# Attention and a routed expert layer on one core: GpSimd's two-operand work waits for VectorE's, row lists come by one copy each, and the plan has new dates

## The chip, the cores and the metric

One Trainium2 chip; the kernel runs on one of its cores. Five engines work beside each other: TensorE (PE, with its weight loads apart as PEld), VectorE (DVE), ScalarE (ACT), GpSimd (POOL) and SyncE (SP, which issues most transfers). The metric is the device time of one execution in microseconds; of several runs the median counts.

## The reference

Attention over 8 batches, 12 heads, 448 tokens and 64 features, with q and k normalised, and then a mixture of 16 experts (4 groups of 4), each token going to one of them:

```python
q_n, k_n = rmsnorm(q, g_q), rmsnorm(k, g_k)
scores = scale * q_n @ k_n.T
attn = softmax(scores)
x = (attn @ v).transpose(0, 2, 1, 3).reshape(3584, 768)
g, e = argmax(x @ w_group), argmax(x @ w_expert[g])      # one expert for each token
out[t] = g_w[t] * e_w[t] * (relu(x[t] @ w1[g, e]) @ w2[g, e])   # 768 -> 1024 -> 768
```

All inputs and the output are float32.

## The kernel before

Every float32 operand of a matmul is carried as a high and a low 16-bit half, and the product is made of three 16-bit matmuls. So behind each tile stands a subtraction that makes the low half, in which two operands lie in SBUF. These are the operations that the change is about:

- `pl` (L619, in `plan_scores`): the low half of the exponentials, 128x896 for two score blocks, on POOL, in some places on DVE. There are 11 for each of the 16 units, 12 for the first (a unit is half a batch, six heads).
- `vl` (L374, `v_lo`): the low half of v, 128x768, twice for each unit, always on DVE.
- `kn` (L298, `k_lo`), on POOL or DVE; `xhl` (L731, in `plan_finish`), on POOL, for the last units also on DVE; `w1l` and `w2l` (L1389, `w_split`), the low halves of the experts' weights, on DVE.
- in the router's `choices` a chain of small operations on DVE and POOL (`rc`, `rd`, `row` and others).

The attention part takes 16 units through preparation (`plan_prep`), the rows' maxima (`mx`, L534, a DVE reduction of PSUM), scores and exponentials, the product with v (`po`, L664) and a store to `x16`. Token groups are routed between units, and `put` (L1067) writes each token into its expert's list `tab`. Then come jobs of up to 352 tokens of an expert each: POOL copies the rows of the list (`rows`, L1401, L1406, L1410) and gathers the tokens by them (`xg`, L1424), SP transposes them (`mx<-xg`), PE runs `mm1` (L1435) and `mul2` (L1462), and POOL scatters the result (L1481).

The order of work comes from a table. `Flow.add` lists some 2,700 tasks with their dependencies and the buffers that they take; `PLAN` gives each task a date (hundredths of a us; a star puts the task on the second of its two engines), and `Flow.emit` writes the tasks out by date. Each engine then runs its instructions in that order and waits only for data and buffers. The table reaches over the attention part and the first 10 of 18 jobs; the later jobs are dated from it by `Moe.plan`. The dates are an order and no times of the chip.

A list's last block of 64 or 32 tokens is worked on by all 128 partitions: the rows are copied 2 or 4 times under each other, each copy a DMA of its own from POOL:

```python
for q in range(r):
    nc.gpsimd.dma_start(t[q * m:q * m + m, i], self.tab[bass.ds(s + a, m)])
```

Of the kernel before, what the change touches and what calls it, by code (L numbers as in the profile page):

```python
# [63 lines left out]

class Flow:
# [40 lines left out]

    def emit(self, agenda, step):
        at = agenda.at(0)
        for t in self.order():
            at(t.start / step, (lambda t=t: t.f(t.on)) if len(t.engines) > 1 else t.f)  # L110


class Attention:
# [129 lines left out]
    def plan_prep(self, flow, u, B, D):  # L243

        nc = self.nc
# [7 lines left out]
        add = flow.add  # L253
# [127 lines left out]
        else:  # L381
# [16 lines left out]
            for a, e in KV:  # L398
# [4 lines left out]
                kl.append(add(both, lambda g, a=a, e=e: k_lo(g, a, e), [kh], uses=[B["nk"], B["kn"]]))  # L403
# [11 lines left out]
            x = add("POOL", lambda: self.one_row(nc.gpsimd, 0, 0), takes=[B["kb"]]) if u == 3 else None  # L415
# [14 lines left out]
            x = add("POOL", lambda: self.max_row(0, 0), takes=[B["qb"]]) if u == 3 else None  # L430
# [4 lines left out]
        for a, e in ((0, V // 2), (V // 2, V)):  # L435
# [4 lines left out]
            D["v"].append(add("DVE", lambda a=a, e=e: v_lo(a, e), [hi, *D["v"]],  # L440
                              takes=[B["vl"]] if a == 0 else (), uses=[B["nv"], B["vh"]] + ([B["vl"]] if a else [])))
# [138 lines left out]
    def plan_scores(self, flow, u, B, D):  # L580
# [42 lines left out]
        for a, e in self.pairs_of(N, u):  # L623
# [7 lines left out]
            x = flow.add(on, lambda g, a=a, e=e: lo(g, a, e), [x], uses=[bp])  # L631
# [77 lines left out]
    def plan_finish(self, flow, u, B, D):  # L709
# [23 lines left out]
        def st():  # L733
# [8 lines left out]
        y = flow.add(["POOL", "DVE"][::-1 if u == self.U - 1 else 1], lo, [x],  # L742
                     uses=[B["xm"], B["hl"]])
# [3 lines left out]
    def plan(self, flow, router, order):  # L747
# [52 lines left out]
        self.final = add("DVE", lambda: order.final(router.bank), done, takes=[Buffer("psx")])  # L800


class Router:
# [462 lines left out]
class Moe:  # L1266
# [222 lines left out]
    def plan_early(self, flow, attn, router, opens):  # L1489
# [15 lines left out]
        def weights(k):  # L1505
            ks = k if k < 2 else k - 2
            for i in range(len(PC)):
# [363 lines left out]
```

## Time and profile before

| | |
|---|---|
| runs | 1018.06 us median of 3, 1016.33 to 1020.02 |
| profiled execution | 1023.34 us, its span 1021.7 us |
| mean granted TensorE clock | 0.971 |
| busy share of the span | PE 89%, DVE 73%, ACT 60%, POOL 56% |

The shares are means over two unlike halves. Up to about 500 us, in the attention part, DVE and POOL are busy nearly all the time; from 650 us PE is, in the experts' part. A busy engine need not be working: the time in which an instruction has begun and is held up counts as its duration.

### The profile page before, as it was taken

What the parts mean: (1) busy time and instruction counts of PE and PEld (TensorE: products, weight loads), DVE (VectorE), ACT (ScalarE), POOL (GpSimd) and SP (SyncE); (2) the same over time, 40 slices, a digit from 0 to 9 for tenths busy, and PEclk for the clock granted to TensorE, in tenths of its full rate; (3) what the DMA queues carried; (4) which work ended last, traced back from release to release, by engine and by line L of the source; (5) the groups of instructions that cost most, each with busy time, mean ns of one, the idle gap of its engine ahead of it and who ended that gap; (6) DMA issues with size and microseconds to landing.
All of it is one profiled execution on the core that took longest, in us unless ns stands there. A gap on an engine that the chain in (4) does not pass through costs nothing.

```text
span 1021.7 us, 28764 instructions
## 1 busy us (share of the span) xinstructions
PE 913.6 (89%) x11761; PEld 651.9 (64%) x11761; DVE 746.2 (73%) x1002; ACT 617.9 (60%) x952; POOL 577.2 (56%) x490
## 2 busy tenths in 40 slices
PE   2789889999999798987987999899898999999995
PEld 1446556566666465655865866577776687778883
DVE  4999988999999999999754465456657585756520
ACT  4789688788888676666642364446446455546520
POOL 7379798899999798887645333223112231434311
PEclk9999899999999899999998999899999899999998
DMA  5756767787779667556998889799988899998910
GB/s 140 199 150 164 169 165 174 167 196 191 185 145 206 147 167 143 103 114 199 229 213 270 218 278 260 237 332 300 264 261 304 295 242 268 344 269 287 296 51 27
DMA packets 223095, 213.77 MB, mean 209 GB/s; under 512 B 129456, under 2 KB 179622, under 8 KB 222961
## 3 DMA queue, kind: packets, MB, share of 16 engines
q1 hardware_dynamic: 213008, 188.23, 70.6%
q0 software_dynamic: 8608, 22.99, 7.2%
q8 instruction: 93, 1.52, 0.7%
q10 hardware_dynamic: 1344, 0.69, 0.3%
q14 instruction: 42, 0.34, 0.1%
HBM read 145.69 MB, written 23.41 MB: 166 GB/s over the span
## 4 chain that ended last, share of the span: by engine, by line
PE 38%; DMA 19%; DVE 15%; POOL 11%; issue 7%; ACT 6%; SPq 3%; POOLq 0%; DVEq 0%; ACTq 0%
PE ps L1462 15%; PE ps L1435 14%; POOL pl L619 6%; DVE mx L534 5%; DMA xg<-x,tb 5%; DMA mx<-xg 4%; DMA stage<-w 3%; PE po L664 3%; PE pss L603 3%; DVE vl L374 2%; ACT p L613 2%; POOL xhl L731 1%; DMA nq<-q 1%; DVE ss L267 1%; DMA nk<-k 1%
## 5 line engine op out<-in xcount | busy, mean ns | idle before, releaser
L619 POOL TENSOR_TENSOR pl<-p 128x896 f16<-128x896 f32 (+1 forms) x161 | 269.9, 1698 | 40.4 <-ACT p L613 39.8
L1435 PE MATMUL ps<-mx,w1h 128*128 128x256 f16 (+6 forms) x1728 | 248.9, 260 | 21.0 <-DMA mx<-xg 13.9
L1435 PE MATMUL ps<-mx,w1l 128*128 128x256 f16 (+6 forms) x864 | 214.4, 260 | 0.3 <-DVE w1l L1389 0.3
L613 ACT ACTIVATE p<-pss 128x896 f32<-128x896 f32 (+1 forms) x177 | 152.4, 882 | 71.5 <-PE pss L603 54.8
L1435 PEld LDWEIGHTS <-w1h 128*128 128x128 f16 x1728 | 156.8, 99 | 42.3 <-issue 23.7
L534 DVE TENSOR_REDUCE mx<-pmx 128x2 f32<-128x896 f32 (+1 forms) x177 | 174.9, 1033 | 8.5 <-PE pmx L524 4.7
L664 PEld LDWEIGHTS <-p 128*128 128x128 bf16 (+1 forms) x3072 | 144.7, 103 | 52.0 <-issue 37.6
L664 PE MATMUL po<-vh,pl 128*128 128x65 f16 (+1 forms) x1536 | 156.9, 197 | 15.4 <-POOL pl L619 14.8
L1462 PE MATMUL ps<-w2h,hl 128*128 128x384 f16 (+2 forms) x768 | 163.9, 304 | 0.8 <-DVE hl L1444 0.8
L1462 PE MATMUL ps<-w2h,hh 128*128 128x384 f16 (+2 forms) x768 | 164.6, 306 | 0.0
L1462 PE MATMUL ps<-w2l,hh 128*128 128x384 f16 (+2 forms) x768 | 164.1, 304 | 0.0
L664 PE MATMUL po<-vh,p 128*128 128x65 f16 (+1 forms) x1536 | 159.3, 200 | 3.2 <-DVE nk L283 1.2
L664 PE MATMUL po<-vl,p 128*128 128x64 f16 (+1 forms) x1536 | 157.6, 196 | 0.0
L1389 DVE SCALAR_TENSOR_TENSOR w2l<-stage,w2h 128x1536 f16<-128x1536 f32 x64 | 111.5, 1753 | 63.0 <-ACT w2h L1387 63.0
L664 PEld LDWEIGHTS <-pl 128*128 128x128 f16 (+1 forms) x1536 | 128.6, 103 | 18.5 <-POOL pl L619 17.6
L1389 DVE SCALAR_TENSOR_TENSOR w1l<-stage,w1h 128x1536 f16<-128x1536 f32 x64 | 112.3, 1777 | 36.8 <-ACT w1h L1387 36.8
L1462 PEld LDWEIGHTS <-hh 128*128 128x128 f16 (+2 forms) x1536 | 101.4, 101 | 57.7 <-issue 6.0
L1481 POOL DMA_INDIRECT out<-y,tb x23 | 35.4, 1539 | 179.7 <-ACT y L1474 76.5
L1442 ACT ACTIVATE hh<-ps 128x256 f16<-128x256 f32 (+6 forms) x144 | 47.2, 347 | 126.0 <-PE ps L1435 111.3
L1387 ACT ACTIVATE w1h<-stage 128x1536 f16<-128x1536 f32 x64 | 93.5, 1479 | 46.4 <-DMA stage<-w 46.1
L1424 POOL DMA_INDIRECT xg<-x,tb x41 | 61.0, 1487 | 105.3 <-DMA mx<-xg 61.4
L603 PE MATMUL pss<-qa,kt 128*128 128x448 f16 x288 | 105.2, 365 | 9.4 <-DVE mx L534 5.0
(208 smaller groups left out, 1611.9 us busy)
## 6 DMA issues: line engine op xcount, KB each, us to landing
stage<-w SPq DMA_DIRECT2D x64, 768.0 KB
stage<-w SPq DMA_DIRECT2D x64, 512.0 KB
stage<-w SPq DMA_DIRECT2D x64, 256.0 KB
vn<-v SPq DMA_DIRECT2D x16, 576.0 KB
x<-xhl SPq DMA_DIRECT2D x16, 576.0 KB
nk<-k SPq DMA_DIRECT2D x30, 288.0 KB
nq<-q SPq DMA_DIRECT2D x30, 288.0 KB
qa<-qh SPq DMA_DIRECT2D x30, 176.0 KB
```

The source lines that it names most:

```text
L534: nc.vector.tensor_reduce(d["mx"][:, a:ns[-1] + 1:step], d.pop(("mm", a))[:, 0:len(ns), 0:448], axis=AX.X, op=ALU.max)
L603: nc.tensor.matmul(s[:, n - a, 0:448], w[:, n * P:(n + 1) * P], mv[:, x:z], start=first, stop=not first)
L613: nc.scalar.activation(p[:, 0:e - a], s, AF.Exp, scale=1.0 / 64)
L619: ENG[eng].tensor_tensor(l[:, 0:n], p[:, 0:n], h[:, 0:n], op=ALU.subtract)
L664: nc.tensor.matmul(o[op, c, 0:nn], w, mv, start=st, stop=sp, skip_group_check=True)
L1387: self.nc.scalar.activation(hi, t, AF.Copy, scale=64.0)
L1389: self.nc.vector.scalar_tensor_tensor(lo, t, 64.0, hi, op0=ALU.mult, op1=ALU.subtract)
L1424: self.nc.gpsimd.indirect_dma_start(g[0:m], None, self.x16[0:n], bass.IndirectOffsetOnAxis(ap=tb[0:m, i, 0:1], axis=0), bounds_check=n - 1 ...
L1435: nc.tensor.matmul(s[:, 0:c], wb[w][:, i, fs], x[:, l + i, o:o + c], start=i + j == 0, stop=i == DC - 1 and j == 2)
L1442: self.nc.scalar.activation(hh, s[:, 0:c], AF.Relu)
L1462: nc.tensor.matmul(s[q * m:q * m + m, 0:n], self.h[h][:, f, a:a + m], wb[w][:, f, o:o + n], start=f + j == 0, stop=f == self.FC - 1 and j ...
L1481: i = self.nc.gpsimd.indirect_dma_start(out, bass.IndirectOffsetOnAxis(ap=idx, axis=0), d.pop(("y", i))[:, 0:self.D // r], None, bounds_ch ...
```

## The change

First, some 360 tasks are marked with `port`: those of POOL with two operands in SBUF, and DVE's of the same kind (`pl`, `vl`, `kn`, `xhl`, the weights' low halves of the planned jobs, some of the router's steps). When `emit` writes out a marked task of DVE, it keeps its last DVE instruction; the next marked task of POOL in the plan then waits by semaphore for that one. One DVE operation is waited for once, and DVE waits for nothing more than before. In the plan 50 tasks of POOL get such a wait, all in the attention part.

Second, a list's last rows come by one copy whose source names them r times. Over the program the copies of such blocks become 18 in place of 50 (8 at L1401, 42 at L1410).

Third, all dates of `PLAN` are new, and with them the order on every engine. By the stars, 10 `pl` of 128x896 and two pairs of `xhl` go from POOL to DVE, and one `kn` of 128x448 from DVE to POOL. The task that sorts the experts (`order.final`) needs only the router's last step in the plan, and no longer the `put`s behind it.

```diff
@@ class Flow
+    def shared(self, task):
+        task.port = True
+        return task
+
     def emit(self, agenda, step):
-        at = agenda.at(0)
+        at, tc = agenda.at(0), self.tc
+        sync = mybir.DependencyInfo(mybir.DependencyClass.Sync, mybir.DependencyReason.SCHED_ONLY)
+        seen, held = [], []
+        def run(t):
+            del seen[:]
+            tc.nc.push_inst_callback(lambda i, *_, **__: seen.append(i))
+            t.f(t.on) if len(t.engines) > 1 else t.f()
+            tc.nc.pop_inst_callback()
+            if t.port and t.on == "DVE":
+                held[:] = [i for i in seen if i.engine == mybir.EngineType.DVE][-1:]
+            elif t.port and held:
+                i = next(i for i in seen if i.engine == mybir.EngineType.Pool)
+                tc.add_manual_dep(i, held.pop().name, sync, reason="one of the two at a time")
+
         for t in self.order():
-            at(t.start / step, (lambda t=t: t.f(t.on)) if len(t.engines) > 1 else t.f)
+            at(t.start / step, lambda t=t: run(t))
...
@@ plan_scores
-            x = flow.add(on, lambda g, a=a, e=e: lo(g, a, e), [x], uses=[bp])
+            x = flow.shared(flow.add(on, lambda g, a=a, e=e: lo(g, a, e), [x], uses=[bp]))
...
@@ Attention.plan
-        self.final = add("DVE", lambda: order.final(router.bank), done, takes=[Buffer("psx")])
+        self.final = add("DVE", lambda: order.final(router.bank), done[:1], takes=[Buffer("psx")])
...
@@ Router.plan
+            x.port = on == "POOL" or j in (1, 3, 5, 6, 12, 15, 18)
...
@@ Moe.rows
-                for q in range(r):
-                    nc.gpsimd.dma_start(t[q * m:q * m + m, i], self.tab[bass.ds(s + a, m)])
+                self.copies(t[:, i], self.tab[bass.ds(s + a, m)], r)
...
-            for q in range(r):
-                nc.gpsimd.dma_start(t[q * m:q * m + m, i], tab[:, a:a + m].rearrange("o p t -> p (o t)"))
+            self.copies(t[:, i], tab[:, a:a + m].rearrange("o p t -> p (o t)"), r)
+
+    def copies(self, dst, src, r):
+
+        m = src.shape[0]
+        self.nc.gpsimd.dma_start(dst, src.unsqueeze(0).to_broadcast([r, m, 2]))
...
 PLAN = """
-210 487 1965 426 1206 1507 11957 13909 2150 1783 2461 0 1 424 485 486 550 849 915 1020 1207 1508 2149* 2354 2567 1444
+210 487 2972 1086 1206 1517 10553 13066 13060 916 3554 0 1 424 485 474 550 731 915 1020 1085 1469 1534* 1779 1898 1442
...
```

POOL in the attention part, where the scores of unit 10 are made (`pl10_2` is its block 2; `p3210_2` the exponentials that it reads; what an instruction waits for stands in brackets). Before:

```order
L619 TENSOR_TENSOR pl10_2_6587<-p3210_2_6586 128x896 [waits Activation_49,Pool_49]
L619 TENSOR_TENSOR pl10_0_6623<-p3210_0_6622 128x896 [waits Activation_49]
L619 TENSOR_TENSOR pl10_10_6657<-p3210_10_6656 128x896 [waits Activation_49]
L619 TENSOR_TENSOR pl10_6_6685<-p3210_6_6684 128x896 [waits Activation_49,Pool_49]
L619 TENSOR_TENSOR pl10_8_6632<-p3210_8_6631 128x896 [waits PE_49]
```

The same place of POOL in the changed kernel:

```order
L637 TENSOR_TENSOR pl10_2_6499<-p3210_2_6498 128x896 [waits DVE_49,Activation_49,Pool_49]
L1084 DMA tab_58<-row_241,slot0_5421 59392x2 [waits DMASW1_49]
L637 TENSOR_TENSOR pl10_4_6630<-p3210_4_6629 128x896 [waits DVE_49,Activation_49]
L637 TENSOR_TENSOR pl10_10_6637<-p3210_10_6636 128x896 [waits Activation_49]
L1084 DMA tab_58<-row_241,slot0_5421 59392x2 [waits DMASW2_49]
L637 TENSOR_TENSOR pl10_8_6686<-p3210_8_6685 128x896 [waits Activation_49]
L749 TENSOR_TENSOR xhl9_6760<-xm9_6363,xhl9_6760 128x3x384 [waits DMAHW5_49,DMAHW4_49,DMAHW6_49,DVE_49,Activation_49]
```

Before, `pl` followed `pl` with no wait for DVE. Now three of these rows wait for DVE, blocks 0 and 6 are gone to DVE, and over the whole program 70 rows of POOL name DVE among their waits, in place of 30.

DVE at the same place, around the first `vl` of unit 11 and the end of unit 9. Of the kernel before:

```order
L283 TENSOR_TENSOR nk13_5953<-nk13_5953,po0_111 128x448
L669 TENSOR_SCALAR rr9_2_6680<-po1_112 128x7
L670 RECIPROCAL rr9_2_6680<-rr9_2_6680 128x7
L534 TENSOR_REDUCE mx11_6590<-pmx11_17_6645 128x1
L374 SCALAR_TENSOR_TENSOR vl11_6687<-vn1_134,vh2_132 128x768
L534 TENSOR_REDUCE mx11_6590<-pmx11_14_6689 128x2
```

And of the changed kernel:

```order
L392 SCALAR_TENSOR_TENSOR vl10_5977<-vn0_133,vh1_131 128x768
L706 TENSOR_TENSOR xm9_6363<-po0_111,rr9_1_6483 128x2x3x64
L707 TENSOR_TENSOR xm9_6363<-po0_111,rr9_1_6483 128x64
L392 SCALAR_TENSOR_TENSOR vl11_6578<-vn1_134,vh2_132 128x768
L637 TENSOR_TENSOR pl10_0_6518<-p3210_0_6517 128x896
L296 SCALAR_TENSOR_TENSOR ss13_6266<-ss13_6266,po0_111 128x42
```

The `vl` of unit 11 stands earlier, behind the `xm` of unit 9, and a `pl` follows it that was POOL's.

POOL where the rows of job 1 are fetched (`tb1`; 224 rows are blocks of 128, 64 and 32), before:

```order
L1406 DMA tb1_9544<-tab_58 128x2 [waits DMASW4_49]
L1410 ISA
L1410 DMA tb1_9544<-tab_58 64x2 [waits DMASW5_49]
L1410 ISA
L1410 DMA tb1_9544<-tab_58 64x2 [waits DMASW6_49]
L1410 ISA
L1410 DMA tb1_9544<-tab_58 32x2 [waits DMASW7_49]
L1410 ISA
L1410 DMA tb1_9544<-tab_58 32x2
```

and now:

```order
L1423 DMA tb1_9575<-tab_58 128x2 [waits DMASW4_49]
L1431 ISA
L1431 DMA tb1_9575<-tab_58 128x1x2 [waits DMASW5_49]
L1431 ISA
L1431 DMA tb1_9575<-tab_58 128x1x2 [waits DMASW6_49]
```

Two copies are left of the six for the blocks of 64 and 32 rows (the first piece goes on for two more copies), each over all 128 partitions.

## Rows read from the trace of the kernel before

**Rows 1.** The page, part 1: busy us, share of the span, instructions.

```profile
PE 913.6 (89%) x11761; PEld 651.9 (64%) x11761; DVE 746.2 (73%) x1002; ACT 617.9 (60%) x952; POOL 577.2 (56%) x490
```

**Rows 2.** Three stretches: length, busy PE PEld DVE ACT POOL, clock, DMA share, GB/s.

```profile
50.00:500.00 450.00, 402.05 (x6707) 265.75 (x6706) 420.49 (x568) 346.08 (x588) 389.85 (x279) 0.97 0.72 165
500.00:650.00 150.00, 135.32 (x1553) 101.60 (x1552) 79.90 (x138) 67.67 (x104) 62.93 (x61) 0.96 0.88 249
650.00:1000.00 350.00, 341.89 (x3222) 263.14 (x3220) 210.09 (x240) 173.21 (x214) 94.63 (x83) 0.98 0.90 267
```

**Rows 3.** The chain that ended last, 50 to 500 us, shares by line.

```profile
by line: POOL pl L619 14.7%; DVE mx L534 10.3%; issue 7.1%; PE po L664 6.8%; PE pss L603 5.8%; DVE vl L374 3.5%; ACT p L613 3.4%; POOL xhl L731 3.0%; POOL tab L1067 2.2%; DMA qb<-ql 2.1%; POOL kn L298 2.1%; DMA qa<-qh 1.8%; DVE ss L267 1.6%
```

**Rows 4.** DVE in order of time, 322 to 345 us: start, us, what.

```profile
324.24 0.95 DVE L374 SCALAR_TENSOR_TENSOR vl<-vn,vh 128x768 f16<-128x768 f32 x1
...
330.96 8.04 DVE L374 SCALAR_TENSOR_TENSOR vl<-vn,vh 128x768 f16<-128x768 f32 x1
```

**Rows 5.** POOL in order of time, 326 to 345 us.

```profile
326.48 9.86 POOL L619 TENSOR_TENSOR pl<-p 128x896 f16<-128x896 f32 x6
336.31 1.87 POOL L298 TENSOR_TENSOR kn<-nk,kn 128x896 f16<-128x896 f32 x1
338.34 1.52 POOL L1067 DMA_INDIRECT tab<-row,slot  x1 [0.16 <-issue]
343.94 1.68 POOL L619 TENSOR_TENSOR pl<-p 128x896 f16<-128x896 f32 x1 [4.08 <-ACT p L613]
```

**Rows 6.** DVE in order of time, 98 to 113 us, the second long `vl`.

```profile
103.53 6.20 DVE L374 SCALAR_TENSOR_TENSOR vl<-vn,vh 128x768 f16<-128x768 f32 x1
```

**Rows 7.** DVE in order of time, 394 to 408 us, the third.

```profile
395.98 1.08 DVE L619 TENSOR_TENSOR pl<-p 128x896 f16<-128x896 f32 x1
...
398.17 5.62 DVE L374 SCALAR_TENSOR_TENSOR vl<-vn,vh 128x768 f16<-128x768 f32 x1
```

**Rows 8.** The chain, pieces from 394 to 408 us.

```profile
398.00 7.33 POOL pl L619 x4
```

**Rows 9.** DVE's groups, 50 to 500 us: count, busy us, mean ns, idle before.

```profile
L374 DVE SCALAR_TENSOR_TENSOR vl<-vn,vh 128x768 f16<-128x768 f32 x31 | 59.7, 1924 | 0.0
...
L619 DVE TENSOR_TENSOR pl<-p 128x896 f16<-128x896 f32 x13 | 16.9, 1304 | 0.7 <-ACT p L613 0.7
...
L731 DVE TENSOR_TENSOR xhl<-xm,xhl 128x1152 f16<-128x1152 f32 x2 | 4.2, 2110 | 0.0
```

**Rows 10.** POOL's groups, 50 to 500 us.

```profile
L619 POOL TENSOR_TENSOR pl<-p 128x896 f16<-128x896 f32 x146 | 254.2, 1760 | 38.4 <-ACT p L613 37.9
L731 POOL TENSOR_TENSOR xhl<-xm,xhl 128x1152 f16<-128x1152 f32 x13 | 31.7, 2436 | 0.2 <-ACT xhl L727 0.2
...
L731 POOL TENSOR_TENSOR xhl<-xm,xhl 128x192 f16<-128x192 f32 x13 | 10.0, 770 | 0.0
```

**Rows 11.** POOL in order of time, 455 to 660 us.

```profile
460.39 0.98 POOL L1180 CAST first<-oof 1x2 int32<-1x2 f32 x1 [0.20 <-DVE oof L1178]
...
532.27 3.47 POOL L1401 DMA_DIRECT2D tb<-tab  x6 [2.15 <-DMA tab<-row,slot]
539.76 1.13 POOL L1424 DMA_INDIRECT xg<-x,tb  x1 [4.01 <-DMA tb<-tab]
...
568.29 2.27 POOL L1410 DMA_DIRECT2D tb<-tab  x4
...
614.51 2.02 POOL L1410 DMA_DIRECT2D tb<-tab  x4
```

**Rows 12.** POOL's groups over the span, the copies of row lists.

```profile
L1410 POOL DMA_DIRECT2D tb<-tab x42 | 22.1, 539 | 2.8 <-DMA out<-y,tb 1.7
L1406 POOL DMA_DIRECT2D tb<-tab x16 | 9.7, 603 | 0.7 <-issue 0.4
...
L1401 POOL DMA_DIRECT2D tb<-tab x8 | 4.2, 532 | 2.5 <-DMA tab<-row,slot 2.1
```

**Rows 13.** Who waited for whom on POOL: us in total, times, longest.

```profile
POOL xg L1424 <- DMA tb<-tab: 6.5, 2, 4.0
```

More of the change, by code (lines that the diff above doesn't have):

```diff
@@ L402, in plan_prep @@
                          takes=[B["kn"]] if a == 0 else (), uses=[B["nk"]] + ([B["kn"]] if a else []))
-                kl.append(add(both, lambda g, a=a, e=e: k_lo(g, a, e), [kh], uses=[B["nk"], B["kn"]]))
+                kl.append(flow.shared(add(both, lambda g, a=a, e=e: k_lo(g, a, e), [kh], uses=[B["nk"], B["kn"]])))
             for a, e in HV:
@@ L414, in plan_prep @@
                 self.got(D, "kmv", a, e, kt[-1])
-            x = add("POOL", lambda: self.one_row(nc.gpsimd, 0, 0), takes=[B["kb"]]) if u == 3 else None
+            x = flow.shared(add("POOL", lambda: self.one_row(nc.gpsimd, 0, 0), takes=[B["kb"]])) if u == 3 else None
             self.got(D, "kcp", 0, N, add("SP", k_cp, [*kt, x], takes=[] if x else [B["kb"]], uses=[B["kt"]] + ([B["kb"]] if x else [])))
@@ L429, in plan_prep @@
             self.got(D, "qa", 0, N, add("SP", qa_mv, evs, takes=[B["qa"]], uses=[B["qh"]]))
-            x = add("POOL", lambda: self.max_row(0, 0), takes=[B["qb"]]) if u == 3 else None
+            x = flow.shared(add("POOL", lambda: self.max_row(0, 0), takes=[B["qb"]])) if u == 3 else None
             self.got(D, "qb", 0, N, add("SP", qb_mv, [*los, x], takes=[] if x else [B["qb"]], uses=[B["qh"]] + ([B["qb"]] if x else [])))
@@ L439, in plan_prep @@
             D["init"].append(hi)
-            D["v"].append(add("DVE", lambda a=a, e=e: v_lo(a, e), [hi, *D["v"]],
-                              takes=[B["vl"]] if a == 0 else (), uses=[B["nv"], B["vh"]] + ([B["vl"]] if a else [])))
+            D["v"].append(flow.shared(add("DVE", lambda a=a, e=e: v_lo(a, e), [hi, *D["v"]], takes=[B["vl"]] if a == 0 else (),
+                                          uses=[B["nv"], B["vh"]] + ([B["vl"]] if a else []))))
     def plan_first(self, add, D, B, N, F, both, d):
@@ L741, in plan_finish @@
         x = flow.add("ACT", hi, D["x"], takes=[B["hl"]], uses=[B["xm"]])
-        y = flow.add(["POOL", "DVE"][::-1 if u == self.U - 1 else 1], lo, [x],
-                     uses=[B["xm"], B["hl"]])
+        y = flow.shared(flow.add(["POOL", "DVE"][::-1 if u == self.U - 1 else 1], lo, [x], uses=[B["xm"], B["hl"]]))
         D["st"] = [flow.add("SP", st, [y], uses=[B["hl"]])]
@@ L1513, in weights @@
                 x = add("ACT", lambda k=k, i=i, st=st: self.w_split(wb(k), PC[i], self.stage[st], 0), [x, m1 if k == 0 else m2, *free], uses=[b])
-                x = add("DVE", lambda k=k, i=i, st=st: self.w_split(wb(k), PC[i], self.stage[st], 1), [x], uses=[b])
+                x = flow.shared(add("DVE", lambda k=k, i=i, st=st: self.w_split(wb(k), PC[i], self.stage[st], 1), [x], uses=[b]))
                 sets[k].append(x)
@@ new lines @@
+14416 14432 14728 15509 4202 4103 4567 5093 4187 5402 5422 5676 5856 6214 6909 5952 6332 7181 6796 7180 7782 7860 8365
+8504 8068 9288 7481 7588 7781 7778 7779 8026 9037 7689 8424 10188 11093 11408 11353 13120 11075 11084 11085 11713
+11966 11968 11089 11094 11354 11502 11579 11765 11969 11983 12083 11356 11489 12333 12509 13061 13132 13248 13716*
+13063 13065 13715 13245 13341 13718 13525 13633 13862 13611 13714 14074 13687 13805 13904 13807 13886 14244 14675
+14767 14871 14872 14877 15041 15045 15213 15368 15267 15325 15508 14246 14418 14422 14424 14428 14435 14519 14726
@@ new lines @@
+44226 44283 44499 44600 44669 44782 45042 45045* 45234 45262* 45397 35534 33518 35881 36606 36090 36801 37124 37325
+38563 38735 38804 40461 40627 40785* 38852 40629 40302 40385 41066 41315 41529 40854 41160 41161 41279 41366 41440
+41713 43526 40722 41316 44487 42228 44599 42110 42286 42353 43525 43579 43679 43140 43228 43328 42518 42701 42852
+42947 43028 43128 42321 42453 43863 43985 44170 44601 44709 45041* 44378 44489 44708 44706 44857 44960 44853 44959
+45237 45157 45281 45396 45044 45236 45645 45651 45741 45840 45399 45646 45650* 45967 45971 46070 45970 46078 46348
@@ L1817 @@
+72994 73111 73112 73168 73215 73262 73672 73674 74082* 74173 74174 74492 74575
 """
```

126 lines of the change are left out of this document (67 added, 59 removed), and 145 rows, old and new, of the table PLAN.

## The prediction

> **What bounds the kernel now.** I read the page first: no engine is busy for the whole span, PE with 89% most of all [rows 1]. So I cut the span into stretches [rows 2]. From 650 to 1000 us PE is busy for 341.9 of 350 us, and the end is PE's: whatever comes before shifts it, and nothing of this change makes a matmul there shorter. From 500 to 650 us PE has 14.7 us of gaps, between the first experts' jobs. From 50 to 500 us, the attention part, DVE is the fullest engine, 420.5 of 450 us; PE has 402.1, POOL 389.9, ACT 346.1. The chain of that stretch changes hands all the time: POOL's `pl` has 14.7% of it, the reduction `mx` 10.3%, PE's `po` and `pss` 6.8 and 5.8%, `vl` 3.5% [rows 3]. No engine binds alone there; the fullest, DVE, is what I count by.
>
> DVE's busy time isn't all work. In order of time one `vl` takes 0.95 us at 324.24, and the next takes 8.04 us at 330.96 [rows 4]. Around the second, POOL runs six `pl` without a pause, each 1.64 us, then a `kn`, until 338.18, and `vl` ends 0.8 us behind that, about its free duration [rows 5]; it has sat through the rest of the third `pl`, three more and the `kn`, five operations. So `vl` waited for a pause of POOL, with its data there and its instruction begun; the first gap that POOL left, where it turned to a DMA, let it through. The same is seen at 103.53 (6.20 us) and 398.17 (5.62 us) [rows 6, 7].
>
> [...]
>
> **The change part by part, in the time of the profiled execution** (1023.34 us; the median of the runs is 1018.06, or 0.9948 of it, and I scale at the end).
>
> *What the waits return to DVE.* In the stretch 31 `vl` are busy for 59.7 us [rows 9]. At the free 0.95 us they would take 29.5, so 30.2 us are spent in being held. The 13 `pl` on DVE take 16.9 us, and at 1.08 us free [rows 7] they would take 14.0: 2.9 us held. The two `xhl` take 4.2; at `pl`'s rate (1152/896 of 1.08, an estimate) 2.8: 1.4 held. Together 34.5 us, the upper bound, which would need that DVE never finds POOL at work. The lower bound is the three long waits alone, 8.04 + 6.20 + 5.62 less three times 0.95, 17.0 us: these are waits behind several POOL operations, which a POOL that stops for the `vl` can't make; the shorter ones are waits for the rest of one operation, and no semaphore of this change stands against those, since DVE itself waits for nothing new. Between them the new order decides, which may or may not put a `vl` where POOL pauses. I take the middle, 25.8 us.
>
> *What moved work costs DVE.* Ten `pl` come from POOL at 1.08 us, 10.8; two pairs of `xhl` at 1344/896 of 1.08, 3.2; one half `kn` goes, -0.5. Together 13.5 us more for DVE. POOL is rid of ten `pl` at 1.68 [rows 5] and two pairs at 2.44 + 0.77 [rows 10], and gets the `kn` (about 1.0): 22.2 us less. What hides this on DVE now is its idle time, 29.5 us of the stretch; but that idle time is scattered in small waits, so I give it no cover and count the 13.5 in full (0 if the new order lays it into the gaps).
>
> *What the waits cost POOL.* 50 operations of POOL wait for DVE. A handoff from DVE to POOL took 0.20 us [rows 11]: 10 us. POOL's own held time falls away: 146 `pl` are busy for 254.2 us, at 1.68 they would need 245.3, so 8.9. With 389.9 - 22.2 - 8.9 + 10 POOL has 368.8 us of work, 21 less than now, and that is the cover for waiting at the semaphores: up to 21 us of it leaves POOL as full as it is now. Queued behind a waiting POOL instruction are the next `pl`, `xhl` and `kn`, for which PE's `po`, the stores and the next unit's transposes wait, and `put`s. I take no cost on the path; the other end is the first rival.
>
> *DVE's account.* 420.5 - 25.8 + 13.5 = 408.2, that is 12.3 us less than now; with the same idle time the stretch is shorter by as much. The bounds are 420.5 - 17.0 + 13.5, 3.5 us less, and 420.5 - 34.5 + 0, 34.5 us less, but then PE (402.1 of 450 now, nothing taken from it) would be at 97% of what is left, so I cap the gain at 26 us, where PE would be at 95%, near the 98% that it holds from 650 us on.
>
> *The row lists.* 32 copies fall away at 0.53 to 0.54 us of POOL each [rows 12], 17 us in all; the new copy over 128 partitions is nearest to L1406's 0.60 us, which takes 18 times 0.07, or 1 us, back. Nearly all lies beside PE's work. Where the gathers set the pace of the first jobs, the lists at 532.27, 568.29 and 614.51 would issue 2.3, 1.7 and 1.5 us sooner (6 copies become 2, and 4 become 1, at the rates of their rows) [rows 11]: 5.5 us if PE's gaps closed by all of it, 0 if the gather waits for its buffer anyway, as the transposes in front of most gathers suggest. I take 2.
>
> Whether the one copy lands as fast as several no row shows. POOL's gathers waited for a list's landing twice, 6.5 us [rows 13]; a landing half as slow again would cost at most 3 us there, which I keep for the upper end. [...]
>
> *The rest of the new dates.* They reorder ACT, PE and SP too, and the sort of the experts may come sooner. No row prices an order. It can't return more than the gaps, and the ends of the two ranges hold what it may cost; I take 0.
>
> Sum: 12.3 + 2 = 14.3 us of 1023.34, so 1009.0, and 1003.8 in the scale of the median. I forecast **1004 us**; its own range, by 3.5 + 0 and 26 + 5.5 us, is 987 to 1015.
>
> **The rivals.**
>
> *POOL becomes the bound (slower).* At 398 us, beside the third long `vl`, the chain is on POOL: four `pl`, 7.33 us [rows 8]. POOL at that moment was the later of the two, and a stop for `vl` would have lengthened the path. `pl`, `xhl` and `kn` on POOL hold 19.8% of the chain of the stretch, against 3.5% for `vl` [rows 3]. The price of a wait is the handoff and, if DVE comes late, the whole of its operation: 0.20 + 0.95. From 21/50, or 0.42 us of waiting beside the handoff, POOL is as full as now; at the whole 0.95, 47.5 us of waits, it would be 26.5 us longer than today, and DVE's gain would be paid for in POOL's idle time: 1023.3 + 26.5 - 2, or 1042 in the median's scale. Halfway between, at 0.69 us a wait, 1029. Against it: a wait is for an operation that the plan has put in front of POOL's, so it costs its whole length only where DVE runs late against POOL.
>
> *Nothing changes.* The two engines excluded each other before, too, so that the wait only changes its place, from a held DVE instruction to a stopped POOL one, and the 13.5 us that DVE gets are what POOL is rid of. Only the row lists are left: 1016. For it speaks that the chain is shared by all engines, against it that DVE stood still for 17 us in three places with its next reductions, on which PE's scores hang, queued behind. [...]
>
> *More than forecast.* The held time goes entirely, the gaps of the first jobs close and the order is a better one: under 987.
>
> **How the numbers follow.** The forecast's case gets 0.70, more than forecast 0.08, nothing changes 0.11, POOL as the bound 0.11. A measurement of this kernel can tell 0.3% or 3 us from no change. The forecast's case is faster over nearly all its range, so faster is 0.77; the unchanged case and the forecast's edge give 0.12 within 0.3%; slower is 0.11. For 8 in 10 the range leaves out half of each outer case: 989 to 1020 us.
>
> **What would show it.** In the changed profile: no `vl` over about 3 us, their busy time near 35 us in place of 59.7; DVE about 408 us between the same pieces of work, with `pl` on DVE up by 10; waits of POOL's `pl` for DVE of some 10 to 30 us in all; the first matmul of the experts some 12 us sooner, and the distance from there to the end within 3 us of today's. If `vl` is short and POOL's waits for DVE are over 30 us, the first rival is right; if `vl` still stands for several `pl`, the waits sit at the wrong operations: POOL, running late, still has to do those that the plan puts before the `vl`. If the attention part is shorter but the end isn't, I am wrong in letting the whole of it through to PE.

## The result, and the profile after

| | before | changed |
|---|---|---|
| median, beside each other on one chip | 1019.04 us (4 runs) | 990.98 us (4 runs, 988.27 to 994.14) |
| ratio, 95% interval | | 0.9722 [0.9677, 0.9767] |
| profiled execution, its span | 1023.34 us, 1021.7 us | 991.11 us, 989.5 us |
| mean granted TensorE clock | 0.971 | 0.980 |

The kernel is 28 us faster, twice what was forecast (14 us), and inside the range (989 to 1020). Two things ahead of the prediction have to be put right. The count of POOL's rows that name DVE among their waits, 70 in place of 30, is wrong; what holds is that 31 rows got a wait for DVE that had none, and that the other planned waits fall on rows that waited for DVE before. And the new table also moves 32 operations between ACT and DVE (17 to DVE, 15 to ACT), which are not named there.

The page of the changed kernel, part 1, answers to [rows 1]: PE needs 14.6 us less for the same 11761 matmuls, DVE 19.0 less, POOL 40.7 less.

```profile
PE 899.0 (91%) x11761; PEld 645.7 (65%) x11761; DVE 727.2 (73%) x1017; ACT 615.0 (62%) x950; POOL 536.5 (54%) x445
```

The attention part between the same pieces of work, from 50 us to the first matmul of the experts, which is at 493.9 us before and at 470.8 now. Before (columns as in [rows 2]):

```profile
50.00:493.90 443.90, 395.97 (x6651) 260.29 (x6650) 418.14 (x564) 341.74 (x573) 388.36 (x276) 0.97 0.71 164
```

And after:

```profile
50.00:470.80 420.80, 387.43 (x6648) 257.28 (x6646) 396.48 (x573) 341.11 (x586) 365.87 (x275) 0.98 0.75 173
```

The stretch is 23.1 us shorter, DVE's busy time in it 21.7, POOL's 22.5, PE's 8.5. DVE's idle time is about the same (25.8 us, now 24.3). The experts' part, from there to the start of the last matmul, takes 511.5 us in place of 516.9, and what follows it another 3.7 us less.

DVE's groups, 50 to 500 us, which answer to [rows 9]: `vl` has its free duration in 25 of 32 places; `pl` and `xhl` are more in number and no shorter.

```profile
L392 DVE SCALAR_TENSOR_TENSOR vl<-vn,vh 128x768 f16<-128x768 f32 x32 | 34.1, 1087 | 0.3 <-DMA nq<-q 0.3
L637 DVE TENSOR_TENSOR pl<-p 128x896 f16<-128x896 f32 x23 | 28.1, 1232 | 0.9 <-ACT p L631 0.8
...
L749 DVE TENSOR_TENSOR xhl<-xm,xhl 128x1152 f16<-128x1152 f32 x4 | 9.1, 2276 | 1.9 <-ACT xhl L745 1.9
```

POOL's largest group in the same stretch, to [rows 10], and below it who waited for whom on POOL, 50 us to the first expert matmul (us in total, times, longest):

```profile
L637 POOL TENSOR_TENSOR pl<-p 128x896 f16<-128x896 f32 x136 | 235.2, 1749 | 34.3 <-ACT p L631 12.9 <-DVE vl L392 7.2 <-DVE kn L316 4.5
```

```profile
POOL pl L637 <- ACT p L631: 13.3, 16, 4.3
POOL pl L637 <- DVE vl L392: 7.2, 4, 2.6
POOL pl L637 <- DVE pl L637: 7.1, 4, 2.9
POOL pl L637 <- DVE kn L316: 4.5, 2, 3.1
```

The waits are there, 32.4 us of POOL for DVE in all rows of this view (5.5 us before); but POOL waits less for ACT, 16.6 us in place of 40.6, most of it for the exponentials. Where that matters is seen on PE. Who PE waited for up to its first expert matmul, before:

```profile
PE po L664 <- POOL pl L619: 14.8, 19, 3.3
PE pmx L519 <- DVE mx L534: 6.3, 1, 6.3
PE pss L603 <- DVE mx L534: 5.0, 8, 2.6
PE pkt L303 <- DVE mx L534: 4.1, 1, 4.1
```

And after:

```profile
PE po L682 <- POOL pl L637: 14.4, 25, 2.1
PE po L682 <- DVE pl L637: 2.5, 3, 1.6
...
PE pmx L542 <- DVE mx L552: 1.5, 1, 1.5
```

Over all rows PE's waits for DVE fall from 26.3 to 10.3 us, and its waits for POOL stay (14.8 and 14.4). Together with the 8.5 us that PE is busy less, these 16.0 us are about the 23.1. That is the gain in one place: DVE's reductions come earlier, and POOL's `pl` come no later.

### The profile page after: what moved, and what is told of

Same layout as the page of the kernel before. It is cut to its first block, busy times and chain, and to the rows that moved or that the text cites. A ratio compares the mean times of both kernels' runs of the same rounds, so it can differ in the third digit from the quotient of the medians.

```text
span 989.5 us, 28672 instructions
## 1 busy us (share of the span) xinstructions
PE 899.0 (91%) x11761; PEld 645.7 (65%) x11761; DVE 727.2 (73%) x1017; ACT 615.0 (62%) x950; POOL 536.5 (54%) x445
## 4 chain that ended last, share of the span: by engine, by line
PE 47%; DVE 17%; DMA 17%; POOL 6%; issue 5%; ACT 5%; SPq 3%; POOLq 0%; DVEq 0%; ACTq 0%
PE ps L1456 20%; PE ps L1483 18%; DVE mx L552 6%; DMA mx<-xg 5%; PE po L682 3%; POOL pl L637 3%; PE pss L621 3%; DMA stage<-w 2%; DMA xg<-x,tb 2%; DMA nq<-q 2%; DVE pl L637 2%; ACT p L631 2%; DMA qa<-qh 2%; DMA rx<-x 1%; POOL xhl L749 1%
## 5 line engine op out<-in xcount | busy, mean ns | idle before, releaser
L637 POOL TENSOR_TENSOR pl<-p 128x896 f16<-128x896 f32 (+1 forms) x151 | 250.1, 1677 | 37.7 <-ACT p L631 13.3
L1456 PE MATMUL ps<-mx,w1h 128*128 128x256 f16 (+6 forms) x1728 | 245.2, 257 | 19.2 <-DMA mx<-xg 12.7
L1456 PE MATMUL ps<-mx,w1l 128*128 128x256 f16 (+6 forms) x864 | 211.7, 257 | 0.0
L682 PE MATMUL po<-vh,pl 128*128 128x65 f16 (+1 forms) x1536 | 156.3, 196 | 17.3 <-POOL pl L637 14.4
L682 PEld LDWEIGHTS <-pl 128*128 128x128 f16 (+1 forms) x1536 | 127.6, 102 | 21.6 <-POOL pl L637 18.2
L1405 ACT ACTIVATE w2h<-stage 128x1536 f16<-128x1536 f32 x64 | 93.9, 1478 | 37.4 <-DMA stage<-w 37.4
L621 PE MATMUL pss<-qa,kt 128*128 128x448 f16 x288 | 102.7, 356 | 4.0 <-ACT p L631 2.4
```

Of the source, the lines that this page charges most:

```text
L621: nc.tensor.matmul(s[:, n - a, 0:448], w[:, n * P:(n + 1) * P], mv[:, x:z], start=first, stop=not first)
L637: ENG[eng].tensor_tensor(l[:, 0:n], p[:, 0:n], h[:, 0:n], op=ALU.subtract)
L682: nc.tensor.matmul(o[op, c, 0:nn], w, mv, start=st, stop=sp, skip_group_check=True)
L1405: self.nc.scalar.activation(hi, t, AF.Copy, scale=64.0)
L1456: nc.tensor.matmul(s[:, 0:c], wb[w][:, i, fs], x[:, l + i, o:o + c], start=i + j == 0, stop=i == DC - 1 and j == 2)
```

## The experiments

e1 to e4, e5 to e8 and e9 to e12 were each measured on one chip beside the kernel before, so the ratios compare across the groups better than the medians. All have the one copy for the row lists except e4. The table puts them together. "Engines" says whether the operations that the new plan moves between POOL and DVE are moved (the 32 between ACT and DVE go with the dates); "start" is the first expert matmul; DVE's busy time is from the windows view up to there, its idle time the rest; the next three columns are sums of all rows of the waits view from 50 us to there. All in us.

| | dates | engines | waits | start | DVE busy | DVE idle | PE for DVE | PE for POOL | POOL for DVE | median | ratio to before |
|---|---|---|---|---|---|---|---|---|---|---|---|
| before | old | old | none | 493.9 | 453.4 | 40.5 | 26.3 | 14.8 | 5.5 | | 1 |
| e3 | old | old | none | 488.6 | 447.4 | 41.2 | 21.8 | 16.1 | 10.9 | 1015.2 | 0.9957 |
| e6 | old | old | with room | 487.6 | 431.4 | 56.2 | 10.4 | 23.0 | 20.8 | 1014.5 | 0.9911 |
| e2 | old | old | all | 505.9 | 428.0 | 77.9 | 8.3 | 46.9 | 60.9 | 1034.3 | 1.0146 |
| e8 | old | new | none | 505.7 | 452.7 | 53.0 | 31.1 | 11.4 | 17.7 | 1037.0 | 1.0161 |
| e10 | old | new | all | 512.6 | 437.1 | 75.5 | 14.2 | 36.7 | 62.5 | 1040.0 | 1.0151 |
| e1 | new | new | none | 489.9 | 452.0 | 37.9 | 30.6 | 9.5 | 20.9 | 1011.8 | 0.9939 |
| e5 | new | new | behind `vl` | 478.2 | 434.4 | 43.8 | 14.8 | 11.9 | 17.7 | 1002.6 | 0.9809 |
| e11 | new | new | with room | 476.0 | 429.6 | 46.4 | 12.0 | 12.8 | 29.2 | 1005.0 | 0.9818 |
| changed | new | new | all | 470.8 | 432.0 | 38.8 | 10.3 | 14.4 | 32.4 | 991.0 | 0.9722 |
| e4 (several copies) | new | new | all | 469.5 | 431.6 | 37.9 | 10.8 | 13.5 | 30.9 | 989.7 | 0.9722 |
| e9 | new | old | all | 496.5 | 421.4 | 75.1 | 12.9 | 27.5 | 31.8 | 1024.8 | 0.9994 |
| e7 | new | new | both ways | 523.9 | 413.4 | 110.5 | 49.6 | 5.9 | 60.8 | 1048.1 | 1.0268 |
| e12 (`vl` of one operand) | new | new | none | 482.5 | 425.4 | 57.1 | 19.1 | 4.0 | 9.3 | 1004.2 | 0.9812 |

**The first four take the parts apart.** e1 has the new dates and engines without the waits:

```diff
-                tc.add_manual_dep(i, held.pop().name, sync, reason="one of the two at a time")
+                held.pop()
```

> The changed kernel (990.98 us) without the semaphore waits: new dates and one copy for each list's last rows stay. If the waits carry the gain (my theory: POOL running on past a held DVE operation is what lost the time), the low halves of v are held up behind several POOL operations again, their busy time rises from 34.8 us towards 50 or more, and the time is 1003 to 1015 us. If the new order carries it (rival: the dates put POOL's pauses where DVE needs them, and the waits are hardly ever the last thing that POOL waits for), the time stays within 988 to 995 us and v's low halves stay under 40 us.

Measured: 1011.79 us, 0.9939 [0.9902, 0.9977]. The time is that of my theory, its cause is not: without the waits no `vl` takes over 2.63 us, and all of them take 43.2, between the two theories. The new order alone did away with the long `vl`. What is held in e1 is `xhl`, up to 9.93 us, and the router's `rd`, up to 6.12. DVE's groups over the span in e1:

```profile
L392 DVE SCALAR_TENSOR_TENSOR vl<-vn,vh 128x768 f16<-128x768 f32 x32 | 42.6, 1351 | 0.3 <-ACT vh L386 0.3
L749 DVE TENSOR_TENSOR xhl<-xm,xhl 128x1152 f16<-128x1152 f32 (+1 forms) x8 | 16.5, 2106 | 4.3 <-ACT xhl L745 4.3
L1040 DVE TENSOR_TENSOR rd<-rc,rcm 128x140 f32<-128x140 f32 (+2 forms) x5 | 8.2, 1639 | 0.2
```

and in the changed kernel (its `vl` as above, 34.1):

```profile
L749 DVE TENSOR_TENSOR xhl<-xm,xhl 128x1152 f16<-128x1152 f32 (+1 forms) x8 | 11.7, 1498 | 1.9 <-ACT xhl L745 1.9
L1040 DVE TENSOR_TENSOR rd<-rc,rcm 128x140 f32<-128x140 f32 (+2 forms) x5 | 2.0, 399 | 0.2
```

e2 has the waits under the old table (`PLAN` of the kernel before, nothing else):

> The dates of before with the semaphore waits and the one copy. If the waits carry the gain, the long waits of v's low halves (8.0, 6.2 and 5.6 us) are gone, their busy time falls from 60.6 to about 40 us and the time to 998 to 1006 us. If the order carries it, the held time of DVE comes back as waits of POOL at the semaphores, and the time is 1012 to 1020 us, or up to 1030 if POOL stops where the old order has not foreseen it.

Measured: 1034.27 us, 1.0146 [1.0090, 1.0201], slower than before. e3 has the edits of both, so that only the one copy is left of the change:

> The dates of before, no waits, only the one copy for each list's last rows. Mine: 2 us sooner than before, 1015 to 1018 us, since POOL's issues lie beside other work but for some 2 us. [...] If the copies carry the experts' part of the gain (5 us of the 28 came between the experts' first matmul and their last), 1011 to 1014 us.

Measured: 1015.24 us, 0.9957 [0.9924, 0.9990]. And e4 undoes the one copy alone:

```diff
-        self.nc.gpsimd.dma_start(dst, src.unsqueeze(0).to_broadcast([r, m, 2]))
+        for q in range(r):
+            self.nc.gpsimd.dma_start(dst[q * m:q * m + m], src)
```

> The changed kernel with the several copies of before: new dates and waits stay. The other side of the copies' question: within 2 us of the changed kernel, 990 to 994 us, if they are hidden; 995 to 998 us if they carry what the experts' part gained; 986 to 990 us if the one copy's landing is late.

Measured: 989.65 us, 0.9722 [0.9682, 0.9762], as the changed kernel; e3 shows 0.1 to 0.8% for the copies. So the copies carry little, the waits alone cost (e2 against e3), the dates alone return little, and only together they give 2.8%.

e2's trace shows how the waits can cost. The old table puts a `vl` 0.01 us ahead of a `kn` of POOL. Waits of POOL, from 50 us to the first expert matmul:

```profile
POOL kn L316 <- DVE vl L392: 13.3, 1, 13.3
POOL pl L637 <- DVE vl L392: 10.7, 9, 2.2
POOL xhl L749 <- DVE vl L392: 6.3, 2, 4.0
```

POOL in order of time at the first of them, 40 to 70 us:

```profile
51.26 1.88 POOL L316 TENSOR_TENSOR kn<-nk,kn 128x896 f16<-128x896 f32 x1 [13.32 <-DVE vl L392]
```

DVE there (the `vl` at 50.18 stands at the end of a long run of operations without a pause; it is not held, 0.95 us):

```profile
45.52 3.08 DVE L552 TENSOR_REDUCE mx<-pmx 128x2 f32<-128x896 f32 x3
48.51 0.95 DVE L392 SCALAR_TENSOR_TENSOR vl<-vn,vh 128x768 f16<-128x768 f32 x1
49.38 0.88 DVE L301 TENSOR_TENSOR qp<-nq,po 128x704 f32<-128x704 f32 x1
50.18 0.95 DVE L392 SCALAR_TENSOR_TENSOR vl<-vn,vh 128x768 f16<-128x768 f32 x1
51.05 0.81 DVE L301 TENSOR_TENSOR qp<-nq,po 128x640 f32<-128x640 f32 x1
57.42 1.09 DVE L552 TENSOR_REDUCE mx<-pmx 128x2 f32<-128x896 f32 x1 [5.56 <-PE pmx L537]
```

And PE, 47 to 60 us:

```profile
53.19 1.67 PE L321 MATMUL pkt<-i,kn 128*128 128x128 f16 x14 [6.63 <-POOL kn L316]
...
55.03 0.58 PE L621 MATMUL pss<-qb,kb 128*128 128x448 f16 x1
55.41 0.58 PE L621 MATMUL pss<-qa,kt 128*128 128x448 f16 x1
...
59.74 0.35 PE L621 MATMUL pss<-qa,kt 128*128 128x448 f16 x1
59.93 0.35 PE L621 MATMUL pss<-qb,kb 128*128 128x448 f16 x1
```

The same `kn` in e3, which has the same table and no wait:

```profile
44.92 1.88 POOL L316 TENSOR_TENSOR kn<-nk,kn 128x896 f16<-128x896 f32 x1 [7.82 <-ACT kn L312]
```

Read these fences as one chain. Without the wait POOL waits 7.82 us for its data; with it 13.32 us, until a `vl` that is dated 47.35 and begins at 50.18 has ended at 51.13. So `kn` runs 6.3 us later; PE's transposes of it wait 6.63 us; the maxima that PE then makes come late, and DVE, for which POOL had stood aside, is itself idle for 5.56 us. Over the stretch PE's waits for DVE shrink by 13.5 us against e3 and its waits for POOL grow by 30.8.

**Which waits, and where.** e5 keeps only the waits behind a `vl`, under the new plan:

```diff
             if t.port and t.on == "DVE":
-                held[:] = [i for i in seen if i.engine == mybir.EngineType.DVE][-1:]
+                if t.vl:
+                    held[:] = [i for i in seen if i.engine == mybir.EngineType.DVE][-1:]
```

> New dates, one copy; of the waits only those behind a vl, so that 16 of POOL's rows more than without waits name VectorE, in place of 31. The waits alone lost time and the dates alone gave nothing, so I look for which waits the gain of both hangs on. Theory A: it is the vl, since nearly all held time of the kernel before was theirs (30.2 of 34.5 us); then this is within 0.5% of the changed kernel, 988 to 996 us, with vl near 35 us. Theory B: a wait is worth the same wherever it stands; half of the waits then give about half of the 22 us between the dates alone (1011.8) and the whole (990), 998 to 1004 us. Theory C: pl and the small router operations decide, and this is like the dates alone, 1006 to 1014 us.

Measured: 1002.58 us, 0.9809 [0.9779, 0.9838]: theory B. Half of the waits give 60% of what all give over e1 (0.0130 of 0.0217 in the ratios), although `vl` itself is nearly as free as in the changed kernel (37.3 us in all, there 34.8). e6 goes back to the old table and drops the waits without room:

```diff
-                held[:] = [i for i in seen if i.engine == mybir.EngineType.DVE][-1:]
+                held[:] = [(i, t.start) for i in seen if i.engine == mybir.EngineType.DVE][-1:]
...
-                tc.add_manual_dep(i, held.pop().name, sync, reason="one of the two at a time")
+                x, start = held.pop()
+                if t.start - start >= 0.8:
+                    tc.add_manual_dep(i, x.name, sync, reason="one of the two at a time")
```

> Old dates, one copy; a wait only where the plan dates POOL's operation at least 0.8 us behind VectorE's, 24 planned waits of 52 (15 of POOL's rows more, in place of 31). With all of them the old dates took 1034.3 us, with none 1015.2. Theory A: the loss comes from the pairs that the old plan dates 0.01 to 0.4 us apart, where POOL has to stop for the whole operation; without these the wait gives part of its gain, 1003 to 1012 us, and POOL's waits for vl are under 8 us in the attention part. Theory B: a wait costs by how late VectorE runs against the plan, and the room in the dates doesn't help; then half of the waits cost half of the 19 us, 1021 to 1029 us. Theory C: with fewer waits simply less of both, no difference from 1015 us.

Measured: 1014.54 us, 0.9911 [0.9880, 0.9942]. The loss of e2 is gone, so it did come from the pairs with no room; but a gain of 0.5% over e3 isn't clear of the intervals, which overlap. Theory A is right on the loss and not on the gain, where the time is theory C's. e11 makes the same cut, at 0.6 us, under the new plan:

> The changed kernel without the 11 of its 50 planned waits whose POOL operation is dated less than 0.6 us behind VectorE's. Theory A: these waits stop POOL for a whole operation and cost more than they return; without them 984 to 989 us, better than the changed kernel's 991. Theory B: every wait of the new plan returns its share of 22 us, 11/50 of it is lost, 993 to 998 us.

Measured: 1004.98 us, 0.9818 [0.9788, 0.9848]. Theory A fails, and theory B's range is missed too. These 11 waits, 22% of them, carry 44% of the difference between e1 and the changed kernel (0.0096 of 0.0217). So "room in the dates" is no rule: under the old dates the close pairs cost, under the new ones they return. How is shown in part only: of the 15.4 us between the two profiled executions 5.2 lie ahead of the first expert matmul (476.0 and 470.8), and the rest lies in the experts' part, where the plan has no wait.

**Held time by itself.** e7 lets DVE's marked operations wait for POOL's too, so that marked operations of the two never run at the same time:

```diff
             if t.port and t.on == "DVE":
+                if back:
+                    i = next(i for i in seen if i.engine == mybir.EngineType.DVE)
+                    tc.add_manual_dep(i, back.pop().name, sync, reason="one of the two at a time")
...
-            elif t.port and held:
+            elif t.port:
+                back[:] = [i for i in seen if i.engine == mybir.EngineType.Pool][-1:]
+                if not held:
+                    return
```

> The changed kernel, and VectorE's marked operation also waits by semaphore for POOL's marked one before it in the plan (36 rows of VectorE more). In the changed kernel VectorE's operations are still held for about 16 us and POOL's for about 13. Theory A: a VectorE operation that would be held anyway only waits at another place; held time goes to near 0 on both engines and the time stays within 0.6%, 985 to 996 us. Theory B: POOL runs late against VectorE in many places, and VectorE, on which the maxima and PE's scores hang, then waits for POOL operations that it could have gone before: 1000 to 1015 us, with VectorE's waits for POOL over 15 us in the attention part.

Measured: 1048.10 us, 1.0268 [1.0236, 1.0300]: theory B, by more than it said. All `vl` of e7 (count: shortest, median, longest ns):

```profile
L398 DVE SCALAR_TENSOR_TENSOR vl<-vn,vh x32: 882/958/960, 56.5 to 497.3; 128x768 f16<-128x768 f32 x32
```

and of the changed kernel:

```profile
L392 DVE SCALAR_TENSOR_TENSOR vl<-vn,vh x32: 896/949/2699, 53.8 to 446.7; 128x768 f16<-128x768 f32 x32
```

and who DVE waited for in e7, 50 us to its first expert matmul:

```profile
DVE vl L398 <- POOL pl L643: 30.1, 15, 5.0
DVE pl L643 <- POOL pl L643: 14.4, 7, 2.8
```

With POOL's marked operations kept away no `vl` takes over 0.96 us. This shows that the long ones were held by these operations; in e7 nothing else held a `vl`. It also shows that a busy share is no measure: DVE has the least busy time of all kernels here, 413.4 us, and the latest start. In the changed kernel, where a `vl` might slip in between two `pl`, it took 2.70 us at most and the first expert matmul began at 470.8 us; in e7, where it waited for the `pl` planned ahead of it, it waited 30.1 us in 15 places, and the matmul began at 523.9.

e12 takes the second operand from `vl`, under the new plan and without waits:

```diff
-            nc.vector.scalar_tensor_tensor(d["vl"][:, a:e], d["v"][:, a:e], 64.0, h[:, a:e, 0:64],
-                                          op0=ALU.mult, op1=ALU.subtract)
+            nc.vector.tensor_scalar(out=d["vl"][:, a:e], in0=d["v"][:, a:e], scalar1=64.0, scalar2=None, op0=ALU.mult)
```

> New dates, no waits, one copy, and vl is made of one operand in SBUF (64 v without the subtraction of the high half, so the low half is left out and the output is another; the routing stays about the same, since all of x is scaled alike). Without the waits and with two operands this took 1011.8 us, with vl busy for 43 us. Theory A: an operation with one operand isn't held by POOL; vl takes its free time or less, 32 of at most 30 us in all and none over 1.2 us, and since the held vl are about half of what the waits return (vl alone gave 9 of 22 us), 996 to 1005 us. Theory B: it is held like one with two operands; single vl over 2 us appear, and the time stays within 0.5% of 1012.

Measured: 1004.15 us, 0.9812 [0.9782, 0.9842]. Its `vl`:

```profile
L392 DVE TENSOR_SCALAR vl<-vn x32: 483/680/2034, 55.6 to 459.1; 128x768 f16<-128x768 f32 x32
```

Inconclusive. The time is that of theory A, but ten of 32 still take over 1 us, up to 2.03, and the free duration fell by half, from 0.95 us to 0.48, which alone takes 15 us from DVE. So the run can't say what the holding is worth.

**The moved operations.** e8 moves them under the old dates without waits, by a mark `!` at the table's entries:

```diff
-            t.start, t.on = int(x.rstrip("*")) / 100.0, t.engines["*" in x]
+            t.start = int(x.rstrip("*!")) / 100.0
+            t.on = t.engines[("*" in x) != ("!" in x and "POOL" in t.engines)]
```

> Old dates, no waits, one copy, but the operations that the new plan moves between POOL and VectorE are moved (pl on VectorE 26 in place of 16). Beside the same without the move (1015.2 us). Theory A, as I counted: VectorE is the fullest engine and pays for it in full, 13.5 us, so 1025 to 1030 us. Theory B: VectorE's gaps and the lighter POOL cover it, 1011 to 1018 us. Theory C: POOL was the later engine and its relief shows, under 1010 us.

Measured: 1037.03 us, 1.0161 [1.0131, 1.0190], 2.0% or some 21 us over e3, more than theory A. Of that only 5.3 us are busy time of DVE; 11.8 are its idle time. e9 is the changed kernel with the operations back where they were (the same edit, the other way round), e10 is e8 with the waits:

> The changed kernel (new dates, waits, one copy), but the operations that the new plan moves between POOL and VectorE stay where they were before (pl on VectorE 16 in place of 26). Under the old dates the waits cost 1.9%, under the new ones they return 2.2%; this asks whether it is POOL's lighter load that makes the difference. Theory A: POOL, 22 us lighter, has the room to stand still; with its load back the waits return nothing, and this takes 1010 to 1030 us. Theory B: it is the order; the move matters by its own size at most, 985 to 1005 us. Against the changed kernel's 991.

> Old dates with the new engines and the waits, one copy; beside the same without the waits (1037 us). Theory A, POOL's lighter load is the condition of the waits: they now return some 22 us, 1010 to 1020 us. Theory B, the order is: the waits cost about what they cost under the old dates and engines, 19 us, so 1045 to 1060 us.

Measured: e9 1024.78 us, 0.9994 [0.9963, 1.0025]; e10 1039.96 us, 1.0151 [1.0115, 1.0187]. e9 is theory A: with POOL's load back nothing is left of 2.8%. e10 lies between the two: the waits cost 1.9% under the old dates and engines (e3 to e2), nothing measurable with the new engines (e8 to e10), and return 2.2% with the new dates too (e1 to the changed kernel). As far as these runs go, the moved operations take the cost away, the order makes the gain, and each needs the other. New dates with old engines and no waits were not run, so how much of e9 is the load and how much an order that was made for other engines stays open; nor was a run made that takes the moves between ACT and DVE out of the new dates.

## Why the prediction was right, and where its sizes were not

The direction and the mechanism held: the long `vl` are gone, and what DVE got back reached the end. The size did not, 14 us for 28, and that the time still lies in the range is owed to the range's width. Of the 32 us between the two profiled executions 9 lie behind the first expert matmul, where 2 were forecast.

**What bounds, and the account by DVE.** In this change it closes: DVE 21.7 us less, the stretch 23.1 us shorter. It closes because DVE's idle time stayed as it was, and that was assumed. In six kernels DVE's busy time fell by 16 to 40 us against the kernel before, and the start came later, or sooner by less than half as much (e2, e6, e7, e9, e10, e12). PE's waits for DVE and POOL taken together follow the start more closely: 41.1 us before, 24.7 in the changed kernel, 55 in e2 and e7. One execution is a coarse measure of held time: up to the row lists e3 is the same program as the kernel before, and its `vl` take 52.2 us in place of 60.6, and DVE's busy time up to the first expert matmul is 6.0 us less.

**What the waits return**, taken at 25.8 us, is near in size and came from other groups than I counted. Kernels that differ by the waits alone show some 20 us of DVE's busy time up to the first expert matmul: 452.0 in e1 and 432.0 in the changed kernel, 447.4 in e3 and 428.0 in e2. `vl` did return 25.8 us over the program (60.6 to 34.8), and its busy time and its longest piece, 2.70 us, are as forecast; but in e1, without a wait, it is at 43.2 us with no long piece, so only 8.5 us of that are the waits'. The rest of the waits' return is mostly `rd`, `xhl` and `pl`, 6.2, 4.9 and 3.1 us from e1 to the changed kernel. Against the kernel before, `pl` and `xhl` returned nothing: 1.23 us for a `pl` against 1.30, and one still takes 3.69 us. What I left out are small operations, of the marked ones `kn`, `rc`, `rd` and `row`. Before, 50 to 500 us, in DVE's groups:

```profile
L1019 DVE SCALAR_TENSOR_TENSOR rc<-rd,prio 128x140 f32<-128x140 f32 x3 | 4.1, 1367 | 1.0 <-POOL rd L1015 1.0
L1172 DVE TENSOR_TENSOR ogt<-okey 1x256 f32<-1x256 f32 x1 | 3.3, 3258 | 0.0
L1063 DVE SCALAR_TENSOR_TENSOR row<-ru,rs 128x7 f32<-128x7 f32 x3 | 2.8, 941 | 0.0
```

And after:

```profile
L1190 DVE TENSOR_TENSOR ogt<-okey 1x256 f32<-1x256 f32 x1 | 1.1, 1090 | 0.0
L1036 DVE SCALAR_TENSOR_TENSOR rc<-rd,prio 128x140 f32<-128x140 f32 x3 | 1.0, 320 | 0.0
L1080 DVE SCALAR_TENSOR_TENSOR row<-ru,rs 128x7 f32<-128x7 f32 x3 | 0.8, 283 | 0.0
```

A `row` of 7 columns that takes 0.94 us is a held operation as much as a `vl` of 8 us. Over the program `rc`, `kn`, `ogt`, `row`, `rs` and `wrl` fell by 2.8, 2.4, 2.2, 2.0, 1.2 and 1.2 us, 11.8 in all, 0.5 of it the `kn` that moved. Not all of it is the waits' either: `rc`, `ogt`, `rs` and `wrl` are as short in e1, and the last three are not marked in the diff. My upper bound of 34.5 was none, since it went by three groups.

**The moved work** on DVE was 16.0 us (`pl` 10.4, `xhl` 5.6) in place of 13.5, since the new `xhl` are held too. By groups the account closes with it in full: 25.8 + 11.8 - 16.0 is 21.6 us, about what DVE lost. By runs it reads otherwise: the move costs DVE 5.3 us of busy time under the old dates (e3 to e8) and, with the new dates, 4.6 (e3 to e1), since other operations are held for less; under the old dates it costs 11.8 us of idle time besides. So its price isn't its duration. In these terms the 21.4 us of busy time up to the first expert matmul are 20.0 by the waits, less 4.6 by move and dates, and 6.0 between two executions of the same program.

**The waits cost POOL nothing on the path:** right against the kernel before, where POOL's waits for DVE grew by 26.9 us and PE's waits for POOL not at all; POOL's `pl` waited 22 us for DVE, inside the 10 to 30 forecast. Against e1 the waits have a price, 4.9 us more of PE's waits for POOL (9.5 and 14.4), and a return of 20.3 us of PE's waits for DVE. The sign that I gave for the first rival, a short `vl` and over 30 us of POOL's waits for DVE, was a bad one: the changed kernel has 32.4 us in all rows and is faster, and e1 has 20.9 without a planned wait. The cover that I named, a lighter POOL, is borne out by e9 and e10. The first rival had its mechanism and its price right, 1029 to 1042 us; it holds under the old dates, e2 at 1034 us. The second rival, that the wait only changes its place, is refuted here.

**The row lists** were taken at 2 us, and the times can't tell that from 0 or from 4: e3 is 0.4% faster than the kernel before, and the changed kernel isn't faster than e4. POOL's new copy takes 0.85 us to issue, not the 0.60 of L1406 that I took. On the landing, one line's copies in the changed kernel (issue in ns, then us to landing, shortest, median, longest):

```profile
L1431 POOL DMA_DIRECT2D tb<-tab x18: 706/846/893, 468.8 to 908.7; - x18
...
DMA to landing us min/median/max: 3.9/5.9/9.2
```

Before, the separate copies of L1410 had a median of 6.0 us, and each moved a half or a quarter as much; in e4, in the same order as the new copy, 4.7 us. So the one copy lands some 1.2 us later, as far as the landings are known (10 of 18 copies, and 21 of 50 in e4). POOL's gathers now wait for landings for 17.6 us in place of 6.5 [rows 13] and of 7.0 in e4, and yet e4 is no faster.

What the one copy does return lies at a place that I did not count, the end of the program. There POOL's sequencer runs a last `DRAIN`. Before (shortest, median and longest of three, in ns):

```profile
L1866 POOLq DRAIN  x3: 46/103/4895, 1016.0 to 1021.4; - x3
```

and after:

```profile
L1888 POOLq DRAIN  x3: 46/103/1132, 987.5 to 989.2; - x3
```

The longest takes 4.89 us in the two kernels with the several copies (before, e4) and 0.89 to 1.13 us in the twelve with the one copy. Behind PE's last matmul these two end after 10.6 and 9.9 us, the twelve after 6.9 to 7.9.

**The new dates at 0** was the step with no row behind it, and it failed in kind, not only in size. By themselves they are near 0 (e1 against e3, 0.2%), but only since the order earned back the 21 us that the moved operations cost in the old one (e8), nearly all of them in DVE's idle time (53.0 to 37.9). And they are what the waits need. The new table dates the first expert matmul at 470.0 us and it ran at 470.8; every kernel that lacks one of the three parts, or some of the waits, runs later: e11 476.0, e5 478.2, e1 489.9, e9 496.5. The old table dated it 460.1, and it ran at 493.9. An order made on the assumption that the two engines don't collide holds only if they are kept from it: that is my reading of the table, and no run takes single dates apart.

**Everything passes through to the end:** right, and more came: 5.4 us from the experts' part and 3.7 behind the last matmul, the rest of the 32 us between the two profiled executions. The 3.7 are the one copy's, by the drain above. Of the 5.4, 4.6 are busy time of PE for the same matmuls. The eight kernels with the new dates lie between 505 and 522 us from the first expert matmul to the end of the last, and the six with the old dates between 517 and 520; so single executions can't tell the 5.4 from chance.

## What to carry to other kernels

Before counting what an exclusion returns, list every operation of the two kinds, the small ones too, and compare its mean with its shortest. Afterwards, give to the waits only what a run without them lacks: here that is a third of what `vl` returned. A semaphore in place of a hold is worth as much as the order around it allows (here the waits cost 1.9% under the old dates and engines and returned 2.2% under the new ones): look where the stopped engine is waited for, and whether the operation that it waits for is itself late. An order, an assignment and waits that belong together have to be tested together; here the engines alone lost 2.0% and the waits alone 1.9% against e3.

## What was not expected of the hardware

An operation with one operand in SBUF did not keep its shortest duration either: `vl` of e12 took 0.48 us at the least, 0.68 in the median and up to 2.03. That POOL's operations held it, as they held the `vl` with two operands, is my reading; no run keeps the two engines apart there.

PE's pieces of one size did not keep one pace. In e2, after 6.63 us without a matmul, pieces of 448 columns start 0.38 us apart (55.03, 55.41), later 0.19 (59.74, 59.93), while the granted clock of both stretches is shown as 1.00. Over the attention part the same 6761 matmuls keep PE busy for 409.2 us in the changed kernel, 419.2 before and 429.5 in e7, with a granted clock there of 0.98, 0.97 and 0.93. So some of what DVE's stalls cost, and of what their removal returned, seems to be PE's own time; no run separates it.
